# A float16 product with v for one key tile of six, and ten weight chunks converted later

## The chip, the cores and the metric

One core of a Trainium2 chip runs the whole program. The metric is the device time of one execution in microseconds, as the median of several runs. The engines work side by side, each in the order of its own instruction stream: TensorE (PE; its weight loads are a row of their own, PEld), VectorE (DVE), ScalarE (ACT), GpSimd (POOL) and SyncE (SP), which here issues DMAs.

## The reference, cut to what matters

Three stages follow each other; the output of each is the input of the next.

```
# 1. attention, batch 2, 8 heads, 768 positions, head size 64
mask   = (bucket of 6 sign bits of q @ proj) == (the same of k @ proj)
scores = where(mask, q @ k.T / 8, -1e9); scores -= max
attn   = exp(scores); attn /= sum + 1e-9;  x = attn @ v
# 2. dense layer, 1536 tokens, 512 -> 2048 -> 512
h = x @ w_in;  g = h * tanh(softplus(h));  x = g @ w_out
# 3. eight experts, one for each token (argmax of a router), 512 -> 1024 -> 512
out = gate * (relu(x @ w1[e]) @ w2[e])
```

All inputs are float32, the weights of stage 2 float64 (they come as pairs of 32-bit words). Products are made from two float16 parts of each number, high and low: high x high, high x low and low x high are added in PSUM. One product was an exception: that of the exponentials with v, in float32.

## The kernel before, in words

**Attention.** The 16 heads (batch by batch) are worked through in one stream of groups; group g belongs to head g // 6 and key tile g % 6 (128 of the 768 keys). Each group has six positions, and `run_all` writes out by hand what each engine gets at which position: the table `AT` gives for every helper step of head n its place, counted in positions from the head's first group. `in_order` then fixes this order on every engine. In a group, `score_unit` (L377) makes the scores of a tile with 4 products, and ScalarE makes the exponentials p (L389) into one of `PB` buffers. Three groups later (`PVL`) `pv` (L392) multiplies p with the tile's v, in two halves of the 768 queries (c = 0 and 1), into two PSUM banks that add up over the six tiles. `max_unit` (L332) makes the row maxima of a head ten groups ahead; VectorE reads them (L345, L349). After tile 5 `out` (L410) copies the halves from PSUM on ScalarE: for an even head one copy per half (L423), for an odd head a second one for the row of sums (L425). Half 0 is copied in group 2 of the next head, half 1 at the start of group 3, and only then may the next head use that PSUM bank again: its tile 0 comes in group 3.

**Weight chunks of the dense layer** (16 of w_in, 16 of w_out) are converted from float64 to two float16 parts during attention by a generator, `w1_work` (L665): three VectorE steps per chunk (L694, L696, L676), then two ScalarE operations and a GpSimd subtraction (`w1_free`, L700). A hook after each group takes `CVS` steps, here one, so a chunk takes three groups; its ScalarE work is issued behind the group two after its last step. 31 chunks end in attention; what is left runs in the dense layer with `w1_busy` (L707).

**Dense layer** (`moe1`, L782): three token chunks of 512, 16 blocks each, so steps G = 0 to 47 and three more. A step makes h of a block (12 products, `up`, L767), the activation by ScalarE (L844 to L873), VectorE (L846, L851, L867) and GpSimd (L861), and multiplies the block of three steps before (`GLAG`) with w_out (L825). Up to step 24 h has four PSUM banks, later two; L851 is the last reader of a bank. Between the activation's operations there are six slots a step, handed out by `fill` as `FILL` says: a slot first takes a waiting low part (`lows`, VectorE), else the next piece of side work that is due: remaining weight chunks, then the 16 units of the first expert's weights (`w2_work`, L1103, one in 8 slots, ScalarE L1107 and VectorE L1108), and the routing of a finished token chunk (`route`), which begins in steps 18 and 34 with four roundings on ScalarE (L897) and VectorE (L898). What a slot leaves for ScalarE is issued later in the same step, ahead of these roundings.

Of the kernel before, what the change touches and what calls it, by code (L numbers as in the profile page):

```python
# [24 lines left out]
HS = S // 2  # L25
NB = 6
BIG = float(2.0**28)
PB = 5
EMB0 = -2
BLANK = 4  # L30
CVS = ((5, 99, 1),)
LEAD = 5
UP = {95: 0, 99: 1}
TEND = 101
PRE = {96: 2, 97: 2, 98: 2}
RPB, CVB = 1, 3
STEP = 7
AT = dict(rows_t=-7, rows_in=-7, m_row=-22, bits=-90, max_end=-24, hi=-150, lo0=-130, lo1=-122, dup=-114, in_x=-116, in_m=-84, args=-91, load_kq=-190, load_v=-37, out0=50, out1=54, s_row=55, inv=77, r_out=79, r_in=91, scale=112, xhi=127, xlo=139)
GAP = dict(bits=1, max_end=1, inv=1)
STEPS = dict(bits=3, max_end=2, inv=2)  # L40
FROM = dict(rows_in=1, m_row=4, bits=3, max_end=1, hi=4, lo0=4, lo1=4, dup=4, in_x=4, in_m=4, rows_t=1, args=3, load_kq=6, load_v=2)
UNTIL = dict(rows_t=4, rows_in=4)
EVERY = dict(load_kq=(2, 0), load_v=(2, 0)) | {k: (2, 1) for k in ("inv", "r_out", "r_in", "scale", "xhi", "xlo")}
LAST = ("inv", "r_out", "r_in", "scale", "xhi", "xlo")
SP, MP, OP = 1, (1, 5, 11), (1, 5)
NBUF, NVB, KXB, KMB = 3, 2, 5, 4
NPE = 4
AT3 = dict(x=-105, cx0=-105, cx1=-104, args=-94, m=-81, cm0=-80, cm1=-80, bits=-93, dup=-117)
CP3 = ("dd", "ad")
# [94 lines left out]
class Attn:  # L144
    def __init__(self, tc, ctx, q, k, v, proj, ident, ones, xx, dt, rest):
        self.tc, self.nc = tc, tc.nc
        nc = self.nc
        self.q, self.k, self.v = q, k, v
        self.ident, self.ones = ident, ones
        self.xx, self.rest_pools = xx, rest  # L150
        self.ld = ctx.enter_context(tc.tile_pool(name="ld", bufs=2))
        self.st = ctx.enter_context(tc.tile_pool(name="st", bufs=2))
        self.pp = ctx.enter_context(tc.tile_pool(name="pp", bufs=2))
        self.sm = ctx.enter_context(tc.tile_pool(name="sm", bufs=2))
        self.ou = ctx.enter_context(tc.tile_pool(name="ou", bufs=1))
# [24 lines left out]

        for i in range(NVB):
            vn = cp.tile([P, NJ, 65 + P], F32, name=f"vn{i}")
            nc.gpsimd.memset(vn[:, :, 64:66], 1.0)
            nc.gpsimd.memset(vn[:, :, 66 : 65 + 64], 0.0)
            self.VN.append(vn)
        self.PT, self.pt = [], 0
        self.two = rest[1].tile([P, 2 * (S + 1)], F32, name="p12")
        for i in range(PB):
            if i in (1, 2):
                p = self.two[:, (i - 1) * (S + 1) : i * (S + 1)]  # L190
            else:
                p = self.pp.tile([P, S + 1], F32, name=f"p{i}", bufs=1)
            nc.gpsimd.memset(p[:, S : S + 1], 1e-9 / S)
            self.PT.append(p)

        self.pj = cp.tile([P, 3, NB], F16, name="pj3")
        pr = cp.tile([P, NB], F32, name="pjr")
        C = 1.5 * 2.0**17

        def split():  # L200
            nc.vector.tensor_scalar(self.pj[:, 0], pj, C, C, op0=ALU.add, op1=ALU.subtract)
            nc.vector.tensor_tensor(pr, pj, self.pj[:, 0], op=ALU.subtract)
            nc.vector.tensor_copy(self.pj[:, 1], pr)
            nc.vector.tensor_tensor(pr, pr, self.pj[:, 1], op=ALU.subtract)
            nc.vector.tensor_copy(self.pj[:, 2], pr)

        self.proj = split
# [114 lines left out]
    def vn(self, b, h, rows=None):  # L322
# [2 lines left out]
        t = self.VN[(b * H + h) // 2 % NVB]  # L325
        return t[:, :, i * 129 : i * 129 + D] if rows is None else t[:, rows, i * 65 : i * 65 + (P if i else 65)]

    def load_v(self, b, h):
        for i in range(2):
            self.nc.sync.dma_start(self.vn(b, h + i), self.v[b, h + i].rearrange("(p j) d -> p j d", j=NJ))  # L330
# [46 lines left out]
    def score_unit(self, b, h, t):  # L377
        nc = self.nc
        z = self.Z[b, h]
        kq, m = z["x"], z["m"]  # L380
        ts = slice(t * P, (t + 1) * P)
        s = self.ps_s.tile([P, 2, 512], F32, tag="s", name=f"s_{b}_{h}_{t}")[:, :, 0:HS]
        for c in range(2):
            nc.tensor.matmul(s[:, c, :], kq[:, 0, ts], kq[:, 1, c * HS : (c + 1) * HS], start=True, stop=False)  # L384
        for c in range(2):
            nc.tensor.matmul(s[:, c, :], m[0:97, 0, ts], m[0:97, 1, c * HS : (c + 1) * HS], start=False, stop=True)  # L386
        p = self.PT[self.pt % PB]
        self.pt += 1
        nc.scalar.activation(p[:, 0:S].rearrange("p (c n) -> p c n", c=2), s, AF.Exp, scale=2.0**-11)  # L389
        z["p"].append(p)  # L390

    def pv(self, b, h, t, c):  # L392
# [5 lines left out]
        if t == 0:  # L398
            z["o", c] = self.ps_o.tile([P, HS + 1], F32, tag="o", name=f"o_{b}_{h}_{c}")
        o = z["o", c][0:m, 0 : HS + c]  # L400
        nc.tensor.matmul(o, self.vn(b, h, t), z["p"][t][:, cs], start=(t == 0), stop=(t == NJ - 1))  # L401

    def wide(self, b, h, tag, bufs):

        last = b == B - 1 and h >= H - 2
        name = tag
        pool, tag, bufs = (self.rest_pools[0], "stg", None) if last else (self.ou, tag, bufs)
        return pool.tile([P, S + 1], F32, tag=tag, name=f"{name}_{b}_{h}", bufs=bufs)

    def out(self, b, h, c):  # L410

# [11 lines left out]
        self.nc.scalar.copy(z["w"][r, cx], o[r, 0 : HS + c])  # L423
        if i:
            self.nc.scalar.copy(z["s"][:, cs], o[0:1, 0:HS])  # L425

    def out0(self, b, h):
        self.out(b, h, 0)
# [38 lines left out]
    def run_all(self, bs, hook=None):  # L467
# [47 lines left out]
        for n in range(N):  # L515
            for name, at in AT.items():
# [6 lines left out]
                if name in GAP:  # L523
# [61 lines left out]
NR = CH // P  # L585
GLAG = 3
FILL = (0, 4, 2)
XIN = 2
AHEAD = 21
W2LAG = 8  # L590
# [10 lines left out]
class Moe:  # L601
# [63 lines left out]
    def w1_work(self):  # L665
# [18 lines left out]
        for k in range(2 * NF1 + 1):  # L684
            busy = self.busy
            if old:
                end()
                yield 1
            if k < 2 * NF1:
                i, F = todo[k]  # L690
                nextlow, high = (st[k][:, :, :, u] for u in range(2))
                x = self.cv.tile(st[k].shape[0:3], U32, tag="cv", name=f"cv{i}_{F}")
                hi, lo = (self.wo[u][:, F : F + 1, :] if i else self.wi[u][:, :, F * P : (F + 1) * P] for u in range(2))
                nc.vector.tensor_scalar(x, high, 3, 0x3FFFFFF8, op0=ALU.logical_shift_left, op1=ALU.bitwise_and)  # L694
                yield 1
                nc.vector.scalar_tensor_tensor(x, high, 0xC0000000, x, op0=ALU.bitwise_and, op1=ALU.bitwise_or)  # L696
                yield 1
# [9 lines left out]
    def w1_busy(self, hi, lo, w, sc):  # L707

        nc = self.nc
        nc.scalar.activation(hi, w, AF.Copy, scale=sc)  # L710
        if sc == 256.0:
            self.lows.append(lambda: nc.vector.scalar_tensor_tensor(lo, w, sc, hi, op0=ALU.mult, op1=ALU.subtract))
        else:
            nc.gpsimd.tensor_scalar(w, w, sc, None, op0=ALU.mult)
            nc.gpsimd.tensor_tensor(lo, w, hi, op=ALU.subtract)

    def emb(self, tp, ps):

# [63 lines left out]
    def moe1(self, side, more):  # L782
# [22 lines left out]
        for G in range(N + GLAG):  # L805
# [3 lines left out]
            elif G < N:  # L809
                t, w, u = m[G] = [T(tag, G) for tag in "twu"]  # L810
            new_g = 0 < G < N
            cuts, new = new[NC:], []
            ups = [2, 3, 4, 5] if G == 0 else [G + 2] if 4 <= G <= AHEAD + 1 else [G] if AHEAD + 3 < G < N else []
            if G > AHEAD:
# [32 lines left out]
            fill(FILL[0])  # L847
# [8 lines left out]
            fill(FILL[1])  # L856
# [11 lines left out]
            if G < N:  # L868
                for x in new[:NC]:
                    x(1)  # L870
                fill(FILL[2])
# [400 lines left out]
def moe_attn(ctx, tc, a):  # L1272
# [9 lines left out]
    with ExitStack() as c1:  # L1282
# [6 lines left out]
        work = moe.w1_work()  # L1289
        with ExitStack() as c2, tc.using_default_side("right"):  # L1290
            tmp = c2.enter_context(tc.tile_pool(name="tmp", bufs=1))
            at = Attn(tc, c2, a["q"], a["k"], a["v"], a["proj"], ident, moe.ones, xx, dt, (moe.stg, tl))

            emb = moe.emb(tmp, at.ps_m)

# [88 lines left out]
```

## Time and profile before

| what | value |
|---|---|
| time, median of 3 runs | 682.97 us (682.87 to 683.38) |
| profiled execution | 681.95 us |
| its span, first to last instruction | 680.1 us |
| mean granted TensorE clock | 0.997 |
| TensorE, weight loads | 664.9 us (98%), 377.1 us (55%) |
| VectorE, ScalarE, GpSimd busy | 439.9, 471.0, 154.7 us |

Attention runs to about 243 us, the dense layer to about 500 us, the experts to the end. In a timeline each row has start, duration, engine, line, what is written and read, and in brackets the idle time before it and who ended it. A float32 product leaves two records. Products overlap, so the distance between starts, not the duration, says how long one holds TensorE.

### The profile page before, as it was taken

The numbers are of one execution on the slowest core, as the hardware profiler recorded it, in microseconds if no ns is written. First come the engines' busy times: TensorE is split into PE (matmuls) and PEld (weight loads), VectorE is DVE, ScalarE is ACT, GpSimd is POOL, SyncE is SP. The second block draws the span as 40 slices with busy tenths as digits, with TensorE's granted clock in tenths as the row PEclk, the third lists the DMA queues.
The fourth block names the chain that finished last, engine by engine and source line by source line (L and its number), as shares of the span: only waits on it lengthen the run. The fifth ranks groups of instructions, "written<-read, shape, count | busy, mean of one in ns | idle before, by whom it ended". The sixth has DMA issues, their size and how long they took to land. (4 is left out here: it accounts for less than half of the span.)

```text
span 680.1 us, 10416 instructions
## 1 busy us (share of the span) xinstructions
PE 664.9 (98%) x3890; PEld 377.1 (55%) x3890; DVE 439.9 (65%) x747; ACT 471.0 (69%) x716; POOL 154.7 (23%) x166
## 2 busy tenths in 40 slices
PE   7899999999999999999999999999999999999995
PEld 4555555555555454444444544445467777667772
DVE  6877888898887636766676554545556565566620
ACT  5667677776765778999898777887754555556530
POOL 3131211111121222322343243422422011101011
PEclk9999999999999999999999999999999999999998
DMA  7166886988764303244031010310255999978600
GB/s 232 50 151 152 185 197 159 223 157 196 176 143 139 115 10 141 78 139 141 1 89 36 1 62 1 90 35 2 93 186 191 264 300 290 295 241 264 179 24 22
DMA packets 119771, 92.70 MB, mean 136 GB/s; under 512 B 86788, under 2 KB 99076, under 8 KB 119714
## 3 DMA queue, kind: packets, MB, share of 16 engines
q1 hardware_dynamic: 111442, 80.65, 44.4%
q0 software_dynamic: 2240, 6.31, 3.4%
q10 hardware_dynamic: 6032, 5.01, 2.9%
q8 instruction: 32, 0.52, 0.3%
q14 instruction: 25, 0.20, 0.1%
HBM read 63.44 MB, written 14.24 MB: 114 GB/s over the span
## 5 line engine op out<-in xcount | busy, mean ns | idle before, releaser
L401 PE MATMUL o<-p,vn 128*65 128x384 f32 (+3 forms) x384 | 153.3, 486 | 0.1
L767 PE MATMUL h<-xx,wi 128*128 128x512 f16 x576 | 131.3, 379 | 0.1
L825 PE MATMUL x<-wo,g 128*128 128x512 f16 x576 | 131.2, 379 | 0.0
L389 ACT ACTIVATE p<-s 128x768 f32<-128x768 f32 x96 | 77.4, 807 | 53.0 <-PE s L386 51.4
L825 PEld LDWEIGHTS <-g 128*128 128x128 f16 x576 | 56.3, 98 | 68.0 <-POOL g L861 0.3
L767 PEld LDWEIGHTS <-wi 128*128 128x128 f16 x576 | 56.0, 98 | 67.5 <-issue 0.8
L861 POOL TENSOR_TENSOR g<-w,g 128x512 f16<-128x512 f32 x47 | 55.1, 1172 | 149.6 <-ACT g L860 90.4
L1166 PE MATMUL y<-b,hh 128*128 128x512 f16 (+1 forms) x384 | 84.2, 379 | 0.0
L1152 PEld LDWEIGHTS <-a 128*128 128x128 f16 x768 | 75.1, 98 | 5.3 <-issue 0.2
L345 DVE TENSOR_REDUCE mx<-ms 128x1 f32<-128x512 f32 x96 | 65.7, 687 | 15.8 <-PE ms L344 15.5
L867 DVE SCALAR_TENSOR_TENSOR w<-w,u 128x512 f32<-128x512 f32 x47 | 32.5, 692 | 64.1 <-ACT u L858 64.1
L401 PEld LDWEIGHTS o<-p,vn 128*65 128x65 f32 (+1 forms) x384 | 59.6, 163 | 24.8 <-issue 10.8
L1152 PE MATMUL h<-xt,a 128*128 128x240 f16 x672 | 70.1, 266 | 0.0
L1166 PEld LDWEIGHTS <-hh 128*128 128x128 f16 (+1 forms) x384 | 43.8, 114 | 37.6
L846 DVE SCALAR_TENSOR_TENSOR t<-t,u 128x512 f32<-128x512 f32 x47 | 39.1, 831 | 22.2 <-ACT t L873 22.2
L647 DVE SCALAR_TENSOR_TENSOR b<-st,b 128x1024 f16<-128x1024 f32 x28 | 33.0, 1221 | 25.6 <-ACT b L646 25.6
L1172 POOL DMA_INDIRECT out_dram<-o,row x16 | 16.3, 1020 | 143.0 <-ACT o L1171 128.8
L647 DVE SCALAR_TENSOR_TENSOR a<-st,a 128x1024 f16<-128x1024 f32 x28 | 34.3, 1224 | 21.8 <-ACT a L646 21.5
L386 PE MATMUL s<-tm 97*128 97x384 f16 x192 | 47.0, 325 | 0.0
L384 PE MATMUL s<-tx 128*128 128x384 f16 x192 | 46.8, 325 | 0.0
L349 DVE TENSOR_REDUCE mx<-ms 128x2 f32<-128x512 f32 x48 | 33.0, 687 | 16.0 <-PE ms L348 15.3
L1171 ACT ACTIVATE o<-y,row 128x512 f32<-128x512 f32 (+1 forms) x16 | 11.0, 687 | 42.2 <-PE y L1166 25.5
(185 smaller groups left out, 922.1 us busy)
## 6 DMA issues: line engine op xcount, KB each, us to landing
st<-in_moe_w_dram SPq DMA_DIRECT2D x32, 1024.0 KB, 6.2
stg<-in_moe_w_in_dram SPq DMA_DIRECT2D x16, 512.0 KB, 4.0
stg<-in_moe_w_out_dram SPq DMA_DIRECT2D x16, 512.0 KB, 4.4
xs<-zrow SPq DMA_DIRECT2D x15, 257.0 KB, 7.6
vn<-in_v_dram SPq DMA_DIRECT2D x16, 192.0 KB, 6.5
rb<-rd SPq DMA_DIRECT2D x16, 192.0 KB, 4.2
xr<-row SPq DMA_DIRECT2D x2, 1024.0 KB, 4.6
kq<-in_k_dram ACTq DMA_DIRECT2D x5, 384.0 KB, 4.0
```

The lines of the kernel that those rows point to most:

```text
L345: nc.vector.tensor_reduce(z["mx"][:, j, 0:1], s, axis=AX.X, op=ALU.max)
L384: nc.tensor.matmul(s[:, c, :], kq[:, 0, ts], kq[:, 1, c * HS : (c + 1) * HS], start=True, stop=False)
L386: nc.tensor.matmul(s[:, c, :], m[0:97, 0, ts], m[0:97, 1, c * HS : (c + 1) * HS], start=False, stop=True)
L389: nc.scalar.activation(p[:, 0:S].rearrange("p (c n) -> p c n", c=2), s, AF.Exp, scale=2.0**-11)
L401: nc.tensor.matmul(o, self.vn(b, h, t), z["p"][t][:, cs], start=(t == 0), stop=(t == NJ - 1))
L647: nc.vector.scalar_tensor_tensor(lo, src, sc, hi, op0=ALU.mult, op1=ALU.subtract)
L767: self.nc.tensor.matmul(h, self.wi[wu][:, k, fs], x[:, k, xs], start=(i == 0), stop=(i == 3 * NKT - 1))
L825: nc.tensor.matmul(x2[r], gf[:, gu, rs], self.wo[wu][:, f, :], start=(f == 0 and gu + wu == 0), stop=(f == NF1 - 1 and gu == 1))
L846: nc.vector.scalar_tensor_tensor(t1, t1, 0.75, u1, op0=ALU.add, op1=ALU.mult)
L861: nc.gpsimd.tensor_tensor(g[G - 1][:, 1, :], p1, g[G - 1][:, 0, :], op=ALU.subtract)
L1152: nc.tensor.matmul(h[:, v, :], W[0][wu][:, k, fs], xt[e][:, xu * NKT + k, :], start=(i == 0), stop=(i == 3 * NKT - 1))
L1166: nc.tensor.matmul(y[s][0 : CS[s].stop - CS[s].start], hs[F // 2][:, hu, F % 2, CS[s]], W[1][wu][:, F, :], start=(F == 0 and hu + wu == 0) ...
```

## The change

For key tile 2 (`T16`) of heads 2 to 15 (`N16`) the product with v is made from float16 parts: GpSimd splits v of a pair of heads into `V16` (new function `v16`), ScalarE copies p to float16 and VectorE subtracts to get the low part (new function `p16`, 9 and 13 positions after the tile's group begins), and `pv` issues three float16 products instead of a float32 one. The extra column of p is now 1 and the scaling of that column is done once at the end, on GpSimd. The two float16 parts take the place of one p buffer (`PB` 5 to 4); their memory also serves as p for two tiles of head 0. `CVS` takes 0.7 steps per group, so that 22 chunks end in attention and ten in the dense layer, three slots apart, their low part on VectorE always. Up to step 18 the slots are dealt 3 and 3 instead of 4 and 2. The output rows of the last pair of heads stand in the last chunks of the w_out buffers instead of the staging buffers.

```
-PB = 5
+PB = 4
-CVS = ((5, 99, 1),)
+CVS = ((5, 99, .7),)
+T16 = (2,)
+N16 = range(2, 16)
+    AT: v16=-16, p16=(9, 13)
...
+    def v16(self, b, h):
...
+        for i in range(2):
+            for k, t in enumerate(T16):
+                vh, vl = (x[:, k, i * 129 : i * 129 + D] for x in self.V16[(b * H + h) // 2 % NVB])
+                v = self.vn(b, h + i)[:, t]
+                nc.gpsimd.tensor_copy(vh, v)
+                nc.gpsimd.tensor_tensor(vl, v, vh, op=ALU.subtract)
+    def p16(self, b, h, t, u):
+        hi, lo = (x[:, 0:S] for x in self.P16)
+        p = self.Z[b, h]["p"][t][:, 0:S]
+        if u == 0:
+            self.nc.scalar.copy(hi, p)
+        else:
+            self.nc.vector.tensor_tensor(lo, p, hi, op=ALU.subtract)
...
+        if t in T16 and b * H + h in N16:
+            V = [x[:, T16.index(t), i * 65 : i * 65 + m] for x in self.V16[(b * H + h) // 2 % NVB]]
+            for vu, pu in ((0, 0), (1, 0), (0, 1)):
+                nc.tensor.matmul(o, V[vu], self.P16[pu][:, cs], start=..., stop=...)
+            return
...
-                yield 1
+                yield 3 if busy else 1
...
-        if sc == 256.0:
-            self.lows.append(lambda: nc.vector.scalar_tensor_tensor(lo, w, sc, hi, op0=ALU.mult, op1=ALU.subtract))
-        else:
-            nc.gpsimd.tensor_scalar(w, w, sc, None, op0=ALU.mult)
-            nc.gpsimd.tensor_tensor(lo, w, hi, op=ALU.subtract)
+        self.lows.append(lambda: nc.vector.scalar_tensor_tensor(lo, w, sc, hi, op0=ALU.mult, op1=ALU.subtract))
...
+FILL0, SLOW = (0, 3, 3), 18
+            every = FILL0 if G < SLOW else FILL
```

## Rows read from the trace of the kernel before

**Rows 1.** The page's head.
```profile
span 680.1 us, 10416 instructions
```

**Rows 2.** Windows: stretch, busy us of each engine (instructions), granted clock, DMA share, GB/s.
```profile
40.00:243.00 203.00, 202.75 (x1028) 112.05 (x1026) 167.00 (x329) 144.71 (x220) 38.26 (x32) 1.00 0.70 162
243.00:500.00 257.00, 256.93 (x1301) 118.80 (x1300) 146.33 (x228) 213.49 (x346) 84.84 (x75) 1.00 0.23 69
```

**Rows 3.** Timeline of TensorE in attention.
```profile
202.64 0.81 PE L401 MATMUL o<-p,vn 128*65 128x385 f32 x2
203.29 0.49 PE L384 MATMUL s<-tx 128*128 128x384 f16 x2
203.61 0.49 PE L386 MATMUL s<-tm 97*128 97x384 f16 x2
203.94 0.81 PE L401 MATMUL o<-p,vn 128*65 128x384 f32 x2
```

**Rows 4.** Groups of instructions by form: busy us, mean ns of one, idle before.
```profile
L696 DVE SCALAR_TENSOR_TENSOR cv<-stg,cv 128x512 uint32<-128x512 uint32 x32 | 27.3, 855 | 0.1
L401 PEld LDWEIGHTS o<-p,vn 128*65 128x65 f32 x192 | 25.5, 137 | 14.3 <-issue 6.5 <-ACT su L425 1.1
L676 DVE SCALAR_TENSOR_TENSOR cv<-stg,cv 128x512 uint32<-128x512 uint32 x32 | 24.1, 753 | 0.1
L1108 DVE SCALAR_TENSOR_TENSOR a<-st,a 128x512 f16<-128x512 f32 x8 | 10.2, 1278 | 2.5 <-ACT a L1107 2.5
L465 DVE TENSOR_TENSOR xx<-rb,xx 128x768 f16<-128x768 f32 x8 | 7.6, 948 | 4.6 <-ACT xx L462 4.6
L462 ACT CAST xx<-rb 128x768 f16<-128x768 f32 x8 | 6.5, 816 | 0.0
```

**Rows 5.** Timeline of ScalarE, heads 12 and 15.
```profile
199.24 0.47 ACT L425 COPY su<-o 1x384 f32<-1x384 f32 x1
...
201.04 0.62 ACT L703 ACTIVATE wo<-cv 128x512 f16<-128x512 f32 x1
201.76 0.63 ACT L704 ACTIVATE cv<-cv 128x512 f32<-128x512 f32 x1
...
237.37 1.06 ACT L423 COPY ou<-o 65x384 f32<-65x384 f32 x2
```

**Rows 6.** Timeline of all engines at the start of the dense layer.
```profile
254.52 1.53 DVE L676 SCALAR_TENSOR_TENSOR cv<-stg,cv 128x512 uint32<-128x512 uint32 x1
...
263.01 5.34 PE L825 MATMUL x<-wo,g 128*128 128x512 f16 x24
...
264.27 1.16 POOL L861 TENSOR_TENSOR g<-w,g 128x512 f16<-128x512 f32 x1 [3.07 <-ACT g L860]
```

**Rows 7.** Timeline of TensorE, the products with v in heads 8, 12 and 15.
```profile
148.10 0.81 PE L401 MATMUL o<-p,vn 128*65 128x384 f32 x2
...
200.26 0.81 PE L401 MATMUL o<-p,vn 128*65 128x385 f32 x2
...
238.41 1.46 PE L401 MATMUL o<-p,vn 128*128 128x384 f32 x4
```

**Rows 8.** Timeline of VectorE in head 8.
```profile
146.13 0.69 DVE L345 TENSOR_REDUCE mx<-ms 128x1 f32<-128x512 f32 x1 [0.16 <-PE ms L344]
```

**Rows 9.** Waits: engine and line, what it waited for, us in total, times, longest.
```profile
PEld o L401 <- ACT su L425: 1.1, 2, 0.8
```

**Rows 10.** Timeline of all engines in the dense layer, steps 34 to 36.
```profile
424.12 2.48 DVE L898 SCALAR_TENSOR_TENSOR row<-x,row 128x512 f16<-128x512 f32 x4 [0.24 <-ACT row L897]
...
427.24 0.69 DVE L851 SCALAR_TENSOR_TENSOR w<-t,h 128x512 f32<-128x512 f32 x1
...
427.98 2.75 PE L767 MATMUL h<-xx,wi 128*128 128x512 f16 x12
```

**Rows 11.** Timeline of VectorE and of TensorE, steps 38 and 39.
```profile
442.37 0.69 DVE L851 SCALAR_TENSOR_TENSOR w<-t,h 128x512 f32<-128x512 f32 x1
...
443.51 2.75 PE L767 MATMUL h<-xx,wi 128*128 128x512 f16 x12
```

More of the change, by code (lines that the diff above doesn't have):

```diff
@@ L34 @@
 TEND = 101
+LATE = 12
 PRE = {96: 2, 97: 2, 98: 2}
@@ L37 @@
 STEP = 7
-AT = dict(rows_t=-7, rows_in=-7, m_row=-22, bits=-90, max_end=-24, hi=-150, lo0=-130, lo1=-122, dup=-114, in_x=-116, in_m=-84, args=-91, load_kq=-190, load_v=-37, out0=50, out1=54, s_row=55, inv=77, r_out=79, r_in=91, scale=112, xhi=127, xlo=139)
+AT = dict(rows_t=-7, rows_in=-7, m_row=-22, bits=-90, max_end=-24, hi=-150, lo0=-130, lo1=-122, dup=-114, in_x=-116, in_m=-84, args=-91, load_kq=-190, load_v=-37, out0=50, out1=54, s_row=55, inv=77, r_out=79, r_in=91, scale=112, v16=-16, p16=(9, 13), xhi=127, xlo=139)
 GAP = dict(bits=1, max_end=1, inv=1)
 STEPS = dict(bits=3, max_end=2, inv=2)
-FROM = dict(rows_in=1, m_row=4, bits=3, max_end=1, hi=4, lo0=4, lo1=4, dup=4, in_x=4, in_m=4, rows_t=1, args=3, load_kq=6, load_v=2)
+FROM = dict(v16=2, p16=2, rows_in=1, m_row=4, bits=3, max_end=1, hi=4, lo0=4, lo1=4, dup=4, in_x=4, in_m=4, rows_t=1, args=3, load_kq=6, load_v=2)
 UNTIL = dict(rows_t=4, rows_in=4)
-EVERY = dict(load_kq=(2, 0), load_v=(2, 0)) | {k: (2, 1) for k in ("inv", "r_out", "r_in", "scale", "xhi", "xlo")}
+EVERY = dict(v16=(2, 0), load_kq=(2, 0), load_v=(2, 0)) | {k: (2, 1) for k in ("inv", "r_out", "r_in", "scale", "xhi", "xlo")}
 LAST = ("inv", "r_out", "r_in", "scale", "xhi", "xlo")
@@ L188, in __init__ @@
         for i in range(PB):
-            if i in (1, 2):
-                p = self.two[:, (i - 1) * (S + 1) : i * (S + 1)]
+            if i >= 2:
+                p = self.two[:, (i - 2) * (S + 1) : (i - 1) * (S + 1)]
             else:
                 p = self.pp.tile([P, S + 1], F32, name=f"p{i}", bufs=1)
-            nc.gpsimd.memset(p[:, S : S + 1], 1e-9 / S)
+            nc.gpsimd.memset(p[:, S : S + 1], 1.0)
             self.PT.append(p)
+        self.V16 = []
+        for i in range(NVB):
+            vh, vl = (cp.tile([P, len(T16), 65 + P], F16, name=f"v{u}{i}") for u in "hl")
+            nc.gpsimd.memset(vh, 0.0)
+            nc.gpsimd.memset(vh[:, :, 64:66], 1.0)
+            nc.gpsimd.memset(vl, 0.0)
+            self.V16.append((vh, vl))
+        both = cp.tile([P, 2 * (S + 1)], F16, name="p16")
+        self.P16 = [both[:, u * (S + 1) : (u + 1) * (S + 1)] for u in range(2)]
+        self.PX = both.bitcast(F32)
+        nc.gpsimd.memset(self.PX[:, S : S + 1], 1.0)
         self.pj = cp.tile([P, 3, NB], F16, name="pj3")
@@ L326, in vn @@
         return t[:, :, i * 129 : i * 129 + D] if rows is None else t[:, rows, i * 65 : i * 65 + (P if i else 65)]
+    def v16(self, b, h):
+        nc = self.nc
+        if b * H + h == N16[0]:
+            for u in range(2):
+                nc.gpsimd.memset(self.P16[u][:, S : S + 1], 1.0 - u)
+        for i in range(2):
[11 more added lines that the diff above has]
+            self.nc.vector.tensor_tensor(lo, p, hi, op=ALU.subtract)
     def load_v(self, b, h):
@@ L386, in score_unit @@
             nc.tensor.matmul(s[:, c, :], m[0:97, 0, ts], m[0:97, 1, c * HS : (c + 1) * HS], start=False, stop=True)
-        p = self.PT[self.pt % PB]
+        p = self.PX if self.pt in (0, NJ - 1) else self.PT[(self.pt - 1 - (self.pt >= NJ)) % PB]
         self.pt += 1
@@ L400, in pv @@
         o = z["o", c][0:m, 0 : HS + c]
+        if t in T16 and b * H + h in N16:
+            V = [x[:, T16.index(t), i * 65 : i * 65 + m] for x in self.V16[(b * H + h) // 2 % NVB]]
+            for vu, pu in ((0, 0), (1, 0), (0, 1)):
+                nc.tensor.matmul(o, V[vu], self.P16[pu][:, cs], start=(t == 0 and vu + pu == 0), stop=(t == NJ - 1 and pu == 1))
+            return
         nc.tensor.matmul(o, self.vn(b, h, t), z["p"][t][:, cs], start=(t == 0), stop=(t == NJ - 1))
@@ L405, in wide @@
         last = b == B - 1 and h >= H - 2
-        name = tag
-        pool, tag, bufs = (self.rest_pools[0], "stg", None) if last else (self.ou, tag, bufs)
-        return pool.tile([P, S + 1], F32, tag=tag, name=f"{name}_{b}_{h}", bufs=bufs)
+        if last:
+            w = self.rest_pools[0][tag != "ou"][:, LATE:NF1, :]
+            return w.rearrange("p f d -> p (f d)").bitcast(F32)[:, 0 : S + 1]
+        return self.ou.tile([P, S + 1], F32, tag=tag, name=f"{tag}_{b}_{h}", bufs=bufs)
     def out(self, b, h, c):
@@ L425, in out @@
             self.nc.scalar.copy(z["s"][:, cs], o[0:1, 0:HS])
+            if c:
+                self.nc.gpsimd.tensor_scalar(z["w"][:, S : S + 1], z["w"][:, S : S + 1], 1e-9 / S, None, op0=ALU.mult)
     def out0(self, b, h):
@@ L522, in run_all @@
                     continue
-                if name in GAP:
+                if name == "p16":
+                    for t in T16:
+                        for u in range(2):
+                            put(n, 6 * t + at[u], self.p16, t, u)
+                elif name in GAP:
                     d = GAP[name]
@@ L694, in w1_work @@
                 nc.vector.tensor_scalar(x, high, 3, 0x3FFFFFF8, op0=ALU.logical_shift_left, op1=ALU.bitwise_and)
-                yield 1
+                yield 3 if busy else 1
                 nc.vector.scalar_tensor_tensor(x, high, 0xC0000000, x, op0=ALU.bitwise_and, op1=ALU.bitwise_or)
-                yield 1
+                yield 3 if busy else 1
                 low, old = nextlow, (x, hi, lo, x.bitcast(F32), 256.0 if i else 64.0)
@@ L846, in moe1 @@
                 nc.vector.scalar_tensor_tensor(t1, t1, 0.75, u1, op0=ALU.add, op1=ALU.mult)
-            fill(FILL[0])
+            fill(every[0])
             if new_g:
@@ L855, in moe1 @@
                 nc.scalar.activation(u, w, AF.Square, scale=C1, bias=self.bias[C2])
-            fill(FILL[1])
+            fill(every[1])
             if new_g:
@@ L870, in moe1 @@
                     x(1)
-                fill(FILL[2])
+                fill(every[2])
             if new_g:
@@ L1291, in moe_attn @@
             tmp = c2.enter_context(tc.tile_pool(name="tmp", bufs=1))
-            at = Attn(tc, c2, a["q"], a["k"], a["v"], a["proj"], ident, moe.ones, xx, dt, (moe.stg, tl))
+            at = Attn(tc, c2, a["q"], a["k"], a["v"], a["proj"], ident, moe.ones, xx, dt, (moe.wo, tl))
             emb = moe.emb(tmp, at.ps_m)
```

## The prediction

> **What bounds the kernel now.** I read the span first, then the busy time by stage, then the timeline of each engine around the edited lines. [rows 1, 2]: the span is 680.1 us; TensorE is busy 202.75 of the 203 us of attention (40 to 243) and 256.93 of the 257 us of the dense layer (243 to 500), at a granted clock of 1.00, which is the 2.4 GHz level. So in both edited stages a microsecond of TensorE work taken away is a microsecond gained, and any wait that TensorE newly meets is lost outright. VectorE (167.00 of 203) and ScalarE (213.49 of 257) have room on average; whether they have it at the place where TensorE waits for them must be read from the timeline.
>
> **What is removed.** [rows 3]: a float32 product starts at 202.64 as two records and the next work starts at 203.29, so it holds TensorE 0.65 us. The four float16 score products that follow (same 384 columns, own weights each) take 203.29 to 203.94, 0.65 us for four, 0.1625 us each. The change replaces, for tile 2 of heads 2 to 15 and both column halves, 14 x 2 = 28 float32 products by three float16 ones: 28 x (0.65 - 3 x 0.1625) = 4.55 us less TensorE. No row shows a float16 product with these tiles. From below it is the score product's 0.1625; from above, its weight load is not hidden and adds up to the 0.14 us of the 65-column load [rows 4], 84 x 0.14 = 11.8 us. I take the score product, which also loads new weights each time.
>
> **What is added in attention, and its cover.** ScalarE: 14 copies of the exponentials to float16, 0.816 us each by the same shape [rows 4], 11.4 us; nine weight chunks leave, each 0.62 + 0.63 us [rows 5], 11.3 us. VectorE: 14 subtractions at 0.948 us, 13.3 us; nine times 0.855 + 0.753 us of conversion leave, 14.5 us, beside nine cheaper first steps [rows 4]. So the load is unchanged. GpSimd: four small pieces per pair, at most the 1.16 us of its 128x512 subtraction [rows 6] each, 4.6 us in a pair's 27 us; nobody waits for them until two groups into the next head, and behind them stand only weight conversions, of which it loses nine. I take 0 for them, for the extra fills at the start and for the one-column scaling (its reader comes ten groups later); none of them can gain, and each could cost some tenths. Dropping from five to four buffers costs nothing: the exponential that reuses a buffer follows scores that TensorE issues after the buffer's last product. The product needs the low half late enough: the row maximum ahead of it on VectorE starts at 146.13 and lasts 0.69, the subtraction then ends near 147.7, and the third product of tile 2 would start at 148.10 + 2 x 0.1625 = 148.4 [rows 7, 8]. Margin 0.7 us.
>
> **What is moved inside attention.** This is where I expect half of the gain to go. Before, a chunk takes three groups, so its two ScalarE operations fall always behind groups 0 and 3 of a head. At 0.7 steps per group they drift. Counting the steps through the hook (end of a chunk plus two groups), they fall behind group 2 in heads 2, 7, 12 and 15: between the two halves of the previous head's output copies, and the second half frees the PSUM bank in which TensorE begins the new head's second half. That this wait exists: TensorE's loads waited 1.1 us for these copies in two places already [rows 9]. In head 12 the last copy ends at 199.24 + 0.47 = 199.71 and TensorE uses the bank at 200.26 [rows 5, 7]: 0.55 us in hand, 1.25 us put in front, 0.7 us late, and the 0.14 us weight load starts only then: 0.85 us lost. Head 2 has the same copies: 0.85. In head 15 there are no row maxima left and TensorE is quicker: the copies end at 237.37 + 1.06 = 238.43, the bank is used 0.65 after 238.41, at 239.06; 0.63 in hand, 0.6 late: 0.65 with the load, rounded down. Head 7 follows an even head, whose output has no sum row to copy; there it fits. Sum 2.35 us.
>
> **What is moved into the dense layer.** (a) Its start. The chain that makes the second activated block ends on GpSimd at 264.27 + 1.16 = 265.43, and TensorE wants it after the first twelve of the 24 products that start at 263.01 and last 5.34, at about 265.6 [rows 6]: 0.2 us in hand. The change puts up to four more VectorE pieces (the dearest at 0.855 us, rows 4) among this chain's, and one of them beside GpSimd's subtraction, where this step once took 1.53 us against its mean of 0.753 (254.52, rows 6). Partly they fill gaps in which VectorE waited for ScalarE. Bounds 0 and 1.6; I take 0.6.
> (b) Deadlines. Six slots per step, nine or so per chunk: the last chunk is converted in step 14 and read in step 18; the rows that now live in the output weights' last chunks are read last in step 7, chunk 12 is written in step 8. No stall, and the DMAs that move with the chunks have the DMA engines nearly free.
> (c) The first expert's weights come later. Their 16 units were at slots 18 + 8k; now the chunks come first, and they are at 102 + 8k. Unit 13 so comes to slot 206, in step 34, the step in which the second token chunk is rounded and from which on only two PSUM banks serve h. There VectorE rounds four tiles from 424.12, its product that frees the bank ends at 427.24 + 0.69 = 427.93, and TensorE starts the next block at 427.98, already waiting [rows 10]. Unit 13 puts its ScalarE conversion (0.6) ahead of the roundings and its VectorE part (0.6, GpSimd is idle then) behind them: 1.2 us later, all of it seen.
> (d) Unit 15 falls in step 37, where the bank is free at 442.37 + 0.69 = 443.06 for 443.51 [rows 11]: 0.45 in hand against 0.6 to 0.85 of delay (a unit's VectorE part took 1.278 us behind GpSimd, rows 4): 0.15 to 0.4 late, 0.25. Elsewhere units find VectorE waiting.
>
> **Sum.** 4.55 - (2.35 + 0.6 + 1.2 + 0.25) = 0.15 us, as good as nothing. The profiled execution took 681.95 us (span 680.1 and 1.85 around it), 1.02 below the median of the runs, 682.97; I subtract from the median and predict 682.8.
>
> **The rivals.** *The stalls do not come* (the copies and conversions find gaps, as most units do): 4.55 - 1.0 for the start and a remainder, 679.4; with half of them, 681. For it: TensorE waited almost nowhere before, and ScalarE has gaps of more than 1 us in most groups. Against: in the four places the order on the engine is fixed, and each has under 0.7 us in hand.
> *VectorE late on the low half* (slower): the third product of tile 2 waits in each head. It decides when VectorE is more than 0.7 us behind at group 4. One conversion step held behind GpSimd is worth 0.8 us (1.53 against 0.753), more than the margin; a miss of 0.4 us in each of 14 heads costs 5.6, in half of them 2.8 beside the forecast's losses: 685.6. Against: weight conversions on GpSimd become rarer. The Trainium skill ("SBUF — State Buffer", Who interferes with whom) says that a two-input VectorE operation blocks fully against a GpSimd operation that reads SBUF, whichever starts second waiting; the new subtraction is such an operation. In this trace that shape was never held up (x8 at a mean of 0.948), the conversion step was.
> *The three products are no cheaper* (the change does not do what it says): with an exposed load the gain is 4.55 - 11.8; with half of that exposed, 684.1 plus the stalls, about 687. Against: the score products.
>
> **How the numbers follow.** What a measurement of this kernel can tell from no change is 0.2%, 1.4 us: 681.6 to 684.3. Chances: the forecast 0.45 (its own range 681.2 to 684.2), stalls absent or half of them 0.31, low half late 0.17, products no cheaper 0.07. Faster: 0.30 of the second and 0.06 of the forecast's edge, 0.36. Slower: 0.15 and 0.06, 0.21. Within: 0.43. The range leaves a tenth on each side: 679.0 to 685.6; it holds half of the bound of (a) together with no loss elsewhere, and the low half late in half of the heads.
>
> **What the profile of after would show.** TensorE's products of tile 2 at six per head and 0.49 us per half; loads waiting for the output copies for some 0.8 us in heads 2, 12 and 15; in the dense layer one wait of about 0.3 to 0.9 us at the second activated block and one of 1.4 us two steps after the second rounding, under the line that fills h. Wrong would be: no wait of TensorE above 0.3 us there (then 679 to 680), waits under the tile 2 products (slower), or a stretch of lower clock.

## The result and the profile after

The changed kernel takes 686.62 us (median of 6 runs, 684.69 to 688.56) against 682.86 for the kernel before (6 runs, 682.26 to 683.38): ratio 1.0054, 95% interval 1.0044 to 1.0064. It is slower by 3.8 us. The forecast was 682.8, and the time lies a microsecond above the range. The profiled execution took 684.69 us (span 682.9), 1.9 below the median. Its loss against the profile of before, 2.8 us of span, is accounted for first; why the median lost more, as far as that is known, comes behind it.

The same two windows as in [rows 2]:

```profile
40.00:243.00 203.00, 199.22 (x1051) 111.80 (x1050) 160.65 (x313) 143.50 (x215) 39.54 (x60) 1.00 0.62 138
243.00:500.00 257.00, 255.61 (x1289) 117.89 (x1288) 173.78 (x265) 216.65 (x352) 86.72 (x76) 1.00 0.29 85
```

TensorE was busy all the time before; now 3.8 us of attention and 1.4 us of the dense layer are idle. Conversion work has moved from VectorE's first window (167.00 to 160.65) to its second (146.33 to 173.78). TensorE's timeline shows the new product, one half of tile 2 in head 8:

```profile
149.36 0.33 PE L441 MATMUL o<-p,vh 128*65 128x384 f16 x1
149.52 0.32 PE L441 MATMUL o<-p,vl 128*65 128x384 f16 x1
149.68 0.33 PE L441 MATMUL o<-p,vh 128*65 128x384 f16 x1
149.85 0.38 PE L385 MATMUL ms<-tm 96*128 96x256 f16 x2
```

Three starts in 0.49 us, where [rows 3] had 0.65 us: the gain is there, 28 times 0.16 us, less 0.2 us in head 9 (told below). What TensorE newly waits for (the waits by cause: us in total, times, longest):

```profile
PE o L443 <- ACT su L468: 1.2, 2, 0.6
PE h L813 <- DVE w L898: 1.0, 1, 1.0
PE ms L381 <- DMA tm<-kq: 0.9, 1, 0.9
PE ar L319 <- DMA tx<-ka: 0.8, 1, 0.8
...
PE h L1199 <- DMA xt<-xs: 0.4, 1, 0.4
PE x L872 <- DVE w L898: 0.3, 1, 0.3
PE o L443 <- ACT wo L466: 0.3, 1, 0.3
```

To price each place I set the start of every score, first-layer and expert product against the same product's in the trace of before and read where the difference jumps (places by the time of before):

| place | predicted | after | ScalarE part later | load later | one step per group |
|---|---|---|---|---|---|
| 28 half products | -4.55 | -4.5 | -4.5 | -4.5 | -4.5 |
| output copies, heads 2, 12, 15 | 2.35 | 0.76 + 0.83 + 0.61 | 0 | 0.75 + 0.83 + 0.61 | 0 |
| transposes of tm (head 9) and tx (head 10), 127 to 130 | none | 1.10 + 0.97 | 1.40 | 0 | 0 |
| low half of p late | none | 0.2 | 0.6 | 0.2 | 1.1 |
| start of the dense layer (264) | 0.6 | 0.52 | 0.51 | 0.51 | 0 |
| second rounding (425 to 428) | 1.2 | 0.26 + 0.89 | 0.24 + 0.88 | 0.26 + 0.88 | 0.24 + 0.89 |
| unit 15 (443) | 0.25 | 0 | 0 | 0 | 0 |
| second expert's start (530 to 538) | none | 1.0 | 1.2 | 1.2 | 1.6 |

The last three columns are experiments told below, where "head 10's transposes" stands for the two of the third row. The column of after sums to 2.6 us. At the last expert product the loss is 3.1: 0.3 more come at 53 us, which I did not follow up, and 0.2 in steps of under 0.1 us; what is left of the kernel behind it gives 0.3 back.

**Output copies, as predicted.** Timeline of all engines at the start of head 2:

```profile
58.44 0.47 ACT L468 COPY su<-o 1x384 f32<-1x384 f32 x1
58.81 0.63 ACT L753 ACTIVATE wi<-cv 128x512 f16<-128x512 f32 x1
59.47 0.63 ACT L754 ACTIVATE cv<-cv 128x512 f32<-128x512 f32 x1
60.12 0.48 ACT L466 COPY ou<-o 64x385 f32<-64x385 f32 x1
60.62 0.47 ACT L468 COPY su<-o 1x384 f32<-1x384 f32 x1
...
61.15 0.86 PE L443 MATMUL o<-p,vn 128*65 128x385 f32 x2 [0.55 <-ACT su L468]
```

The chunk's two operations stand between the two halves' copies, and the bank's next user starts when the last copy is done.

**Transposes, not predicted.** Timeline of SP before (start, time that the issue takes), and of all engines in the same stretch of after:

```profile
113.66 0.37 SPq L662 DMA_DIRECT2D stg<-in_moe_w_in_dram  x1
...
116.61 1.46 SPq L247 DMA_TRANSPOSE tm<-kq  x1
118.17 2.08 SPq L247 DMA_TRANSPOSE tx<-ka  x1
```

```profile
115.63 0.34 SPq L712 DMA_DIRECT2D stg<-in_moe_w_out_dram  x1
...
116.69 2.41 SPq L262 DMA_TRANSPOSE tm<-kq  x1
119.19 4.68 SPq L262 DMA_TRANSPOSE tx<-ka  x1
...
127.50 0.42 PE L381 MATMUL ms<-tm 96*128 96x512 f16 x1 [0.94 <-DMA tm<-kq]
...
130.19 0.46 PE L319 MATMUL ar<-pj,tx 128*128 128x18 f16 x12 [0.76 <-DMA tx<-ka]
```

The two issues of L262 by source line, from issue to landing:

```profile
DMA to landing us min/median/max: 10.8/10.9/11.0
```

A chunk's last VectorE step also issues the staging load (512 KB) of a later chunk. At 0.7 steps per group this load drifts too, and here it is issued 1.06 us ahead of head 10's transposes instead of 2.95. They land 10.9 us after their issue (median of the two) instead of 4.4, and TensorE waits for both.

**Low half of p, a rival that came in one head.** Timeline of all engines in head 9:

```profile
161.56 1.15 POOL L755 TENSOR_TENSOR wi<-cv,wi 128x512 f16<-128x512 f32 x1 [0.28 <-ACT cv L754]
161.70 1.84 DVE L363 TENSOR_TENSOR p<-p,p 128x768 f16<-128x768 f32 x1
...
163.22 0.32 PE L441 MATMUL o<-p,vl 128*128 128x384 f16 x1
...
163.59 0.32 PE L441 MATMUL o<-p,vh 128*128 128x384 f16 x1
```

VectorE's subtraction for the low half (L363) starts 0.14 us behind GpSimd's subtraction for a weight chunk (L755) and takes 1.84 us; in the other 13 heads it takes 0.95 or 0.96 and ends 0.5 to 1.3 us before TensorE needs it. Here it ends at 163.54, and the third product starts at 163.59, 0.37 us behind the second instead of 0.16: 0.2 us are lost. The list of waits does not have it, because the records of the products overlap and so show no idle time.

**Dense layer.** Timelines of all engines, at its start and in steps 34 to 36:

```profile
263.90 0.69 DVE L898 SCALAR_TENSOR_TENSOR w<-t,h 128x512 f32<-128x512 f32 x1
...
264.64 0.59 PE L872 MATMUL x<-wo,g 128*128 128x512 f16 x2 [0.35 <-DVE w L898]
...
424.52 0.63 ACT L1154 ACTIVATE b<-st 128x512 f16<-128x512 f32 x1
...
425.05 2.04 ACT L944 ACTIVATE row<-x 128x512 f16<-128x512 f32 x4
...
428.06 0.68 DVE L1155 SCALAR_TENSOR_TENSOR b<-st,b 128x512 f16<-128x512 f32 x1
...
429.37 0.69 DVE L898 SCALAR_TENSOR_TENSOR w<-t,h 128x512 f32<-128x512 f32 x1
...
430.11 1.24 PE L813 MATMUL h<-xx,wi 128*128 128x512 f16 x5 [0.97 <-DVE w L898]
```

At the start the wait is at the fourth product, not the thirteenth: the PSUM bank of the output's second tile was that of block 1's h, and L898 still reads it. At the rounding, unit 13 stands ahead of the roundings on ScalarE (424.52) and ahead of the freeing product on VectorE (428.06), as foreseen.

**Why the median lost more.** In three of the later profiles of this schedule TensorE's granted clock falls right behind the wait for the transposes. Windows of the second profile of the changed kernel:

```profile
126.00:130.00 4.00, 2.04 (x8) 0.78 (x6) 1.23 (x4) 1.29 (x2) 0.00 (x0) 0.93 1.31 161
130.00:132.00 2.00, 2.00 (x18) 0.96 (x17) 1.66 (x4) 1.62 (x3) 0.48 (x1) 0.50 1.16 292
132.00:136.00 4.00, 4.00 (x17) 2.54 (x16) 3.50 (x7) 2.59 (x4) 1.95 (x5) 0.89 0.39 102
```

After a wait of 1.96 us the clock is 0.50 (the 1.2 GHz level), for 3.4 us in all, worth 1.7 us; the jump there is 3.7 instead of 2.1 us. In the profile of after, with 0.94 and 0.76 us of waiting in two pieces, the clock stayed at 1.00. Other executions carry only their mean clock. In the five float16 schedules with this wait it was 0.995 or below in 20 of 36 executions, in the six without it in 4 of 48, and in those of the kernel before, timed beside the experiments, in 12 of 71. (With the float32 product, told below, it was in 0 of 5.) In the changed kernel the two low ones took 688.56 and 687.32 us, the others 684.69 to 686.64; in its second measurement the three low ones took 684.69, 686.97 and 688.45, the others 685.00 to 686.62. So the clock is a part of it, shown in three profiles, and not all: the profiled execution was the fastest of its six, and the four at the higher clock have a median of 686.2. The rest stays open; the second expert's start, which lost 1.0 us in the first profile and 1.7 in the second, can be a part of it.

### The profile page after: what moved, and what is told of

Same layout as the page of the kernel before. It is cut to its first block, busy times and chain, and to the rows that moved or that the text cites. A ratio compares the mean times of both kernels' runs of the same rounds, so it can differ in the third digit from the quotient of the medians.

```text
span 682.9 us, 10559 instructions
## 1 busy us (share of the span) xinstructions
PE 662.4 (97%) x3918; PEld 376.7 (55%) x3918; DVE 462.9 (68%) x770; ACT 475.0 (70%) x721; POOL 158.2 (23%) x201
## 5 line engine op out<-in xcount | busy, mean ns | idle before, releaser
L443 PE MATMUL o<-p,vn 128*65 128x384 f32 (+3 forms) x328 | 131.3, 486 | 1.6 <-ACT su L468 1.2
L443 PEld LDWEIGHTS o<-p,vn 128*65 128x65 f32 (+1 forms) x328 | 51.2, 164 | 25.6 <-issue 10.7
```

## The experiments

All but the ninth were timed in alternation with the kernel before (682.8 to 683.3 us beside them); "again" below is the first. The four groups that were timed together differ by up to 0.5 us in the kernel before, so a difference against again from another group is known no better than that.

**The changed kernel, unedited.**

> The changed kernel once more, unedited, for a second profile. Theory: the losses that the order on an engine fixes come back at the same places and sizes (the first product after the output copies in heads 2, 12 and 15 late by 0.76, 0.83 and 0.61 us, the dense layer's start by 0.5, steps 34 to 36 by 1.15), the one under the transposed keys of head 10 (2.1 us in the first profile) comes from DMA timing and may have another size; time 684.5 to 687.5. Rival, one-off noise: the 2.1 us and the 1.0 us at the second expert are absent and the time is 683 to 684.

686.13 us (684.69 to 688.45), ratio 1.0049 [1.0033, 1.0065]. The same places, the same sizes, but 3.7 us at the transposes, with the fall of the clock shown above, and 1.7 us at the second expert's start instead of 1.0.

**ScalarE part later.** The two ScalarE operations that fall behind group 2 are held until behind group 3.

```
-                behind = parts.pop(0)
+                behind = held + parts.pop(0)
+                held.clear()
+                if 0 <= g and g % 6 == 2:
+                    held.extend(behind)
+                    behind = []
```

> ScalarE's part of a weight chunk that would come behind group 2 of a head comes behind group 3. Theory: TensorE no longer waits for the output copies in heads 2, 12 and 15, 2.2 us less than the changed kernel run beside it, nothing else moves. Rival (the lost time is elsewhere, ScalarE has no room): the wait moves to the exponentials and the gain is under 0.7 us.

684.59 us, ratio 1.0030 [1.0015, 1.0044], 1.5 below again. The trace is clear: the three jumps of 2.2 us are 0, the transposes' wait stays (1.2 us), so the drift behind group 2 is the cause of the first. The intervals of the two ratios overlap; the median moved less than the trace, and six of its twelve executions had a mean clock of 0.995 or below (686.0 us against 683.1 for the other six); the fall of the clock is taken for the reason.

**Load later.** A staging load due behind group 2 or 3 is issued behind group 4.

```
-                st.append(self.w1_load(todo[k + 2][1], todo[k + 2][0]))
...
+                self.loads.append(partial(put, k + 2))
+                if busy or self.at % 6 not in (2, 3):
+                    self.flush()
...
+                if g % 6 == 4:
+                    moe.flush()
```

> A staging load that would be issued behind groups 2 or 3 of a head, just ahead of the transposes of keys and queries on the same queue, is issued behind group 4, after them. Theory: the transposes of head 10 land in time, 2.0 us less (up to 3.5 if other executions lose more there). Rival (the transposes are late by chance, or for their own length): no difference beyond 0.5 us.

683.42 us, ratio 1.0016 [1.0005, 1.0027], 2.7 below again. SP's timeline now, and behind it the time to landing of the two transposes by source line:

```profile
115.88 1.44 SPq L262 DMA_TRANSPOSE tm<-kq  x1
117.41 1.88 SPq L262 DMA_TRANSPOSE tx<-ka  x1
119.35 1.40 SPq L712 DMA_DIRECT2D stg<-in_moe_w_out_dram  x1
```

```profile
DMA to landing us min/median/max: 4.3/5.8/7.4
```

With the load behind the transposes no wait for them is left, and the output copies' jumps stay. This is the step that the prediction lacked.

**Units closer together**, so that none falls in step 34: `W2LAG = 8` becomes 6.

> The units of the first expert's weights come every 6 slots instead of 8, so that the last is done in step 31, ahead of the rounding in step 34. Theory: the waits of steps 34 to 36 fall back from 1.4 to 0.25 us, 1.15 us less. Rival (more side work per step overloads ScalarE or VectorE): new waits of TensorE under the lines that fill h between steps 17 and 31, no gain.

688.47 us, ratio 1.0077 [1.0058, 1.0097]: nothing gained. The waits at 425 to 428 us are gone, but the units now meet the routing of the first token chunk:

```profile
385.22 2.75 PE L813 MATMUL h<-xx,wi 128*128 128x512 f16 x12 [0.66 <-DVE w L898]
...
391.54 0.17 PE L1020 MATMUL rk<-oh,tri 128*128 128x8 f16 x1 [0.97 <-DVE oh L1012]
```

Jumps of 0.81 and 1.11 us, more than the 1.15 saved.

**One step per group.** `CVS = ((5, 99, .7),)` becomes `((5, 71, 1),)`: 22 chunks as in the change, but at the old rate and so at the old places of a head; ten still go to the dense layer.

> One constant: the 22 chunks of attention run at one VectorE step per score group, as before the change, in groups 5 to 70, and the ten others keep their place in the dense layer. The float16 product stays. Every ScalarE part and every staging load then has the place in its head that it had before. Theory (the drift of the chunks inside attention costs 2.2 us at three output copies and some 2.0 us at head 10's transposes): both are gone in the trace, the time is 3.5 to 4.5 us under the changed kernel, about 682.2. Rival (the cost is that attention now holds float16 products and any chunk at all places a stall somewhere): the time stays within 1 us of the changed kernel and the stalls are found at other heads.

681.15 us, ratio 0.9974 [0.9963, 0.9985]: faster than the kernel before, 5.0 below again. Copies, transposes and also the dense layer's start cost 0. Head 10's transposes land in 3.8 us. So these losses came from the rate of 0.7, not from the float16 product or the ten moved chunks. But at the end of attention the products are 3.2 us early and not 4.5: at the old rate VectorE's subtraction meets GpSimd's in six heads (2, 3, 5, 7, 9 and 11) and takes 1.81 to 1.84 us there; the third product is 0.2 us late in five of them, the row maximum behind it 0.1 in head 2. No run moved the subtraction out of GpSimd's way.

**Dense layer alone.** Side work begins at the 15th slot, and a ScalarE part in the rounding's step waits for the next step.

```
-side = [[0, x] for x in side]
+side = [[14, x] for x in side]
-while self.later:
+while self.later and not (new and G > NF1 + GLAG):
```

> Two edits in the dense layer alone: its side work begins at the 15th place of the list instead of the first (2.3 steps later), and a ScalarE part that falls into the step of the second rounding waits for the step behind it. Theory: the wait of 0.35 us at TensorE's 4th product of the first output (0.5 us in all) and the two at 425 and 428 us (0.26 and 0.89) are gone, 1.65 us, and nothing comes late behind them; the time is 684.5. Rival (the chunks and units have a deadline that the delay breaks, or the ScalarE part puts the next step's gelu off as far): the stalls come back one to three steps later, within 0.7 us of the changed kernel. The stalls in attention stay in both.

688.78 us, ratio 1.0081 [1.0063, 1.0099]: the rival. The three waits went, and later jumps of 0.50, 1.11, 1.12 and 0.39 us came at 381, 386, 433 and 454 us.

**Moved conversions alone.** The float32 product for every tile (`N16 = range(99, 100)`), without the splitting of v and p that the float16 product needs (`FROM` of `v16` and `p16` 99 instead of 2), the rest as changed.

> The float32 product with v is kept for every tile and only the conversions are moved, as in the change: the price of the second half of the change by itself. Theory (the product saves 4.5 us wherever it is and the move costs 8): the time is the changed kernel's plus 4.5, about 690.6, and the trace has the stalls at the output copies, head 10's transposes, the dense layer's start and the second rounding, with nothing from the 28 half products. Rival (the shorter products are what makes ScalarE and the transposes late, since TensorE arrives 0.16 us earlier each time): the stalls shrink without them, and the time is under 688.5.

690.25 us, ratio 1.0114 [1.0098, 1.0129], 4.1 above again against 4.5 expected. The jumps at copies, dense layer and rounding are within 0.05 us of those of after; the transposes cost 1.55 us there and another 1.5 at 155 us, and unit 15 costs 0.34 at 443 us. So the rate of conversion costs its stalls without the float16 product too. That the product gives its 4.5 us in either company is shown only by the starts in the traces: the two kernels do not have all stalls in common.

**All cures at once** (ScalarE part and load later, dense layer as above), the rate of 0.7 kept.

> The cures together, the float16 product kept: a chunk's ScalarE part behind group 3 instead of group 2, its staging load behind group 4, the dense layer's side work from the 15th place, and no ScalarE part in the step of the second rounding. Theory: 2.2 at the output copies, 2.0 or more at the transposes, 0.5 at the dense layer's start and 1.15 at the second rounding are gone, the gain of 4.5 stays and about 1 us at the second expert's start remains lost: 679.5, some 3.3 us under the kernel before. Rival (each cured wait uncovers another within a microsecond): 681.5 to 683.

682.94 us, ratio 0.9994 [0.9984, 1.0004]: the rival again. Attention is cured but for the low half, late in heads 7 and 9 (the products are 3.6 us early at 243.6 us), and 3.0 us are lost again between 381 and 454 us.

**The kernel before, profiled again.**

> The kernel before, unedited, for a second profile: whether the second expert's start is late there too. In the first profile five transposes on SP's queue took 6.31 us together and TensorE lost nothing between 530 and 538 us. Theory (the delay of 1.0 to 1.7 us there, in seven of the eight profiles since, belongs to the change): 6.3 us and no wait of TensorE for the transposes. Rival (it comes and goes with the execution, and the first profile was one without): a wait for the transposes of 0.3 to 0.7 us here as well.

One execution, 682.29 us. The five transposes took 6.33 us; TensorE waited 0.2 us for them and lost 0.3 here. The two profiles of before so differ by 0.3 us at this place; the 0.8 us (units closer together) to 2.2 (dense layer alone) of the float16 profiles so far are more than that.

**One step per group, and units 13 to 15 later** by 10 slots, or by 5:

```
-yield lag
+yield lag + (10 if i == 12 else 0)
```

> The aligned kernel (one VectorE step per score group in attention), and in the dense layer the 14th unit of the second expert layer's weights and the two behind it are queued 10 places later: none falls into the steps of the second rounding, 34 and 35. Theory: the waits of 0.24 and 0.89 us at TensorE go and nothing takes their place: 680.0, 1.1 us under the aligned kernel. Rival (as with the lag of 6 and the delayed start, the units then meet another step that has no room): a wait of 0.4 to 1.1 us at step 36 to 38, 681.0.

> As the run before, with 5 places instead of 10: the unit leaves the step of the second rounding but falls into the next, 35, which cuts into nothing and has no product with the rounded rows yet. Theory (the wait at 427.98 us comes from the unit in step 34 alone): both waits gone, 680.0. Rival (ScalarE is behind from the rounding on, and any unit in step 35 costs): the 0.24 us goes, a wait of 0.5 to 0.9 us remains at step 36, 680.7.

By 10: 680.48 us, ratio 0.9962 [0.9951, 0.9974]; no wait at the rounding or behind it. By 5: 681.00, ratio 0.9965 [0.9954, 0.9976]; one jump of 0.52 us one step further on (a wait of 0.34). The two intervals overlap, the traces tell them apart: a unit in step 35 costs half of what it costs in step 34.

**TensorE's instruction fetch.** What stayed open was the second expert's start. Of five transposes that SP issues there, one takes 1.95 us in the trace of after, the others 1.16 to 1.25, and in that stretch one instruction packet lands (SP's timeline; the DMA view of 526 to 528 us; the page's queues for the whole kernel: packets, MB):

```profile
525.52 7.02 SPq L1190 DMA_TRANSPOSE xt<-xs  x5
...
526.73 1.95 SPq L1190 DMA_TRANSPOSE xt<-xs  x1
```

```profile
q8 instruction: 1, 0.02, 3.6%
```

```profile
q8 instruction: 32, 0.52, 0.3%
```

32 packets of 16 KB for 3918 matmuls and as many weight loads, one for every 122 or so: I took them for TensorE's own instructions. The changed product adds matmuls ahead of this place, so every later packet comes earlier. In the trace of before that one came at 536 us. Two runs move the packets by nothing but the number of warm-up matmuls at the start (`warm 12` of 384 columns becomes `warm 60` of 77, or `warm 82` of 56):

> As the run with 10 places, and the 12 matmuls of 384 columns that warm TensorE up at the start become 60 of 77 columns: the same columns, 48 matmuls and weight loads more in TensorE's instruction stream ahead of everything. Theory (TensorE's own instruction fetch, a 16 KB packet on queue 8 every 130 matmuls or so, slows the transpose that SP is issuing): the packet at 521.4 us comes 48 matmuls earlier, about 514, while SP waits for the rows; the five transposes of the second expert take 6.3 us instead of 7.04, TensorE's losses at 530 to 538 fall from 1.6 us to 0.5 to 0.9, and the time from 680.5 to about 679.7. Rival (the slow issue belongs to SP's own stream or to the place in the program): the slow transpose stays among the five and the time stays within 0.3 us.

> The kernel before, with 82 warm-up matmuls of 56 columns in place of 12 of 384: 70 more in TensorE's stream, nothing else. Theory: the packet that came at 536.1 us comes some 9 us earlier and lies among the five transposes of the second expert, one of which takes 1.9 to 2.4 us; the five take 7.0 us or more instead of 6.31, TensorE loses 0.5 to 1.0 us there, and the time is 683.5 to 684. Rival: the five keep 6.31 us and the time stays within 0.3 us of the kernel before.

Away (on top of the run with 10 slots): 679.88 us, ratio 0.9953 [0.9939, 0.9966]. DMA view of 512.5 to 515.5 us, whose first row is the busy share in 40 slices, and SP's timeline:

```profile
DMA  5969800000000000000000000900000000000000
...
q8 instruction: 1, 0.02, 3.0%
```

```profile
515.14 1.09 SPq L1185 DMA_DIRECT2D row<-xs  x2
...
520.62 6.33 SPq L1191 DMA_TRANSPOSE xt<-xs  x5
```

The packet is at 514.4 us, 7 us earlier, as 48 matmuls put it; the five transposes are back at 6.33. The start of the expert costs 0.9 instead of 1.6 us. The time is 0.6 us under the run with 10 slots, but the intervals of the two ratios overlap; it is the traces that tell them apart. What is left at this start without a packet among the five, 0.3 us (kernel before again), 0.7 (moved conversions) and 0.9 (here), begins ahead of them: their row loads start 0.2 to 0.6 us later against TensorE than in the first profile of before. Why stays open. Onto (the kernel before): 684.48 us, ratio 1.0021 [1.0012, 1.0030]. DMA view of 517 to 520 us and SP's timeline:

```profile
q8 instruction: 1, 0.02, 2.9%
```

```profile
518.65 1.72 SPq L1138 DMA_DIRECT2D row<-xs  x2
...
524.77 6.33 SPq L1144 DMA_TRANSPOSE xt<-xs  x5
```

I missed the five: the packet came at 518.6 us and met the two row loads ahead of them, 1.72 us instead of 0.82. The transposes are so 0.9 us late and the expert's start loses 1.4 us more than in the first profile of before, 1.1 more than in the second; 0.6 us more were lost at the kernel's start, as in the run with the units closer together, whose start nobody edited. The expectation's letter fell, its mechanism held: the packet moves with TensorE's count, and the issue of SP that it meets takes 0.7 (a transpose of after) to 0.9 us longer (the row loads here).

The version with one step per group, the units 10 slots later and the 60 warm-ups beats both kernels: 3.1 us under the kernel before, 6.3 under again.

## Why the prediction was wrong

**What is removed: right.** 4.5 us for 4.55; the float16 product costs the score product's 0.16 us, the load stays hidden.

**Added in attention: right but for one head.** The subtraction took 0.95 us (0.948 taken) and kept the margin of 0.7 us in most heads; behind GpSimd in head 9 it took 1.84, and the third product was 0.2 us late. I had set the doubled time against the conversion step alone, because eight operations of the subtraction's shape were never held up in the trace of before. My "against" was right at the rate of 0.7, where one subtraction of 14 is held up; at the old rate six are.

**"What is moved inside attention": this step failed.** Its sum, 2.35 us, was sound as far as it went: 0.76, 0.83 and 0.61 us in the heads named, and 0 when only the ScalarE part was moved. But it counted a drifting chunk as "its two ScalarE operations". The chunk's end also issues a 512 KB load on the queue that carries the transposes, and that load drifted as well. I wrote that "the DMAs that move with the chunks have the DMA engines nearly free" of the dense layer and asked nothing of the kind of attention, where the load came 1.06 us ahead of two transposes: 2.1 us, and 3.7 where the clock fell behind the wait. With the load alone moved the wait is gone. Whether the delay arises on the shared queue or in the DMA engines no run here tells. The Trainium skill (DMA: Bandwidth & Descriptors, Two DMAs through the same engine are not ordered) says that descriptors of one queue on one DMA engine start in order. The times to landing fit that, 10.9 us with the load 1.06 us ahead against 4.4 (2.95 us ahead) and 5.8 (behind), but no run here shows the order itself.

**Dense layer's start: right size (0.52 for 0.6), wrong link.** I followed the chain to the second activated block; the bank that L898 frees is needed nine products earlier. The conversion step beside GpSimd that I feared is there (L726 at 261.33, 1.65 us).

**Second rounding: right**, 1.15 for 1.2, at the two engines named. **Unit 15:** 0 for 0.25; it did fit here, and cost 0.34 in the run of moved conversions.

**Sum.** By the items that I had, 4.5 - 2.2 - 0.5 - 1.15 = 0.65 us faster. Missing were 2.1 us at the transposes, 1.0 at the second expert, 0.3 at 53 us, 0.2 for the low half, and the clock in part of the executions. "A stretch of lower clock" stood among the things that would show me wrong, without a place or a price, and the range held nothing for it: its upper end came from the low half of p late by 0.4 us in half of the heads, and it was late by 0.2 in one.

**The rivals.** The low half in time in 13 heads of 14, the products cheap, the stalls there: none of the three at its price. (That of the third does not add up: 684.1 us and 4.4 us of stalls make 688.5, not 687; the range does not rest on it.) The fourth, a transfer on SP's queue that becomes the bound, was not on the list.

## What to carry to other kernels

When a rate is changed, everything that a step issues drifts against the pattern around it: list all of it, the DMAs too, and set each against its queue's neighbours at every position that it will pass through. A rate that divides the pattern (here one step per group, three to a chunk, six groups to a head) keeps the moved work at places that are known to be free: a single constant turned 0.5% slower into 0.3% faster. It says nothing of work that is new at those places: the new subtraction then met GpSimd in six heads instead of one. And a list of waits by cause is not enough to call a product on time; the distance between starts is. A stall is best cured by moving the one thing that causes it; shifting the whole list, as two runs here did, meets the next tight step.

## What the runs showed of the hardware

During the run 16 KB instruction packets land, one for about 122 matmuls with their loads; they moved with the number of matmuls ahead (48 more, 7 us earlier), so I take them for TensorE's. Of the five transposes at the second expert's start the one that such a packet meets took 1.7 to 2.6 us in ten profiles, the others 1.1 to 1.3 (1.7 instead of 0.8 for two small loads). A place that nobody edited so lost 1.1 to 1.4 us in one run and gained 0.7 in another.

VectorE's subtraction of 128x768 took 1.84 us instead of 0.95 when it started 0.14 us behind a GpSimd subtraction (head 9 of after); where GpSimd's started second (head 4), VectorE's kept its 0.95 us and GpSimd's took 1.32 instead of 1.15.

Transposes issued 1.06 us behind a 512 KB load on the same queue landed 10.9 us after their issue, with the load behind them 5.8. A wait of 1.96 us was followed by half the clock for 3.4 us, waits of 0.94 and 0.76 us were not.
